# An attention, expert and dense kernel on one core: two column groups share a PSUM bank, and four row loads are issued ahead of seven weight loads

## The chip, the core and the metric

The kernel runs on one core of a Trainium2 chip. The core has five engines with instruction queues of their own: PE (TensorE, the matrix multiplier, whose weight loads are shown apart as PEld), DVE (VectorE), ACT (ScalarE), POOL (GpSimd) and SP (SyncE, which here does nothing but issue DMAs). Each of them takes its instructions in the order in which they were written; they wait for one another through semaphores. [...] The metric is the time of one execution on the device in microseconds (us); of several executions the median is given.

## The reference

Three stages follow each other: attention in chunks, a layer of eight experts with one expert for each row, and a dense layer.

```python
B, H, S, D = 4, 8, 768, 64                 # attention: out[c] = softmax(q_c k_ctx^T / 8) v_ctx
x = attn_out.transpose(0, 2, 1, 3).reshape(3072, 512)
# experts: 8, w1 [512, 1024], w2 [1024, 512]
do = x @ w_skip > 0;  xc = x[do];  e_idx = argmax(xc @ w_gate)
for e in range(8):
    h = np.maximum(xc[mask] @ w1[e], 0.0)
    y[mask] = gate_w[mask, None] * (h @ w2[e])
out[do] = xc + y
# dense: w1, w2, w3 [512, 768], w_out [768, 512]
h = np.maximum(np.maximum(x @ w1, x @ w2), x @ w3)
return h @ w_out
```

## The kernel before

Matmuls take fp32 data as pairs of a rounded part ("hi") and the rest ("lo"): a product a·b is three matmuls, hi·hi, lo·hi and hi·lo. ACT makes the hi part, DVE the lo part, of everything that is multiplied.

**Experts** (`experts`, the loop over e). For each expert up to 256 rows were gathered (POOL, L368) and transposed (`trans`, tiles xh and xl). The first layer makes the 1024 hidden columns in eight groups f of 128 columns. One group is 12 matmuls of 256 rows (L433) into a PSUM tile hp; there are four such tiles (bufs=4), each a bank of 512 columns of which a group uses 256. ACT then writes relu(hp) to hh (L434), and DVE writes what is left to hl (L435), which frees the tile for the group four further on. The second layer (`gemm2`, L454) adds up over f, for two halves h of the rows, into the two yp banks (one buffer each): 6 matmuls of 512 columns for each f, which need hh and hl of that f. In the last expert all f of h=0 come first, then those of h=1, with four transposes of loaded rows (L501, from x0, loaded at L442) between them.

The weights come in 64 pieces of 512 KB, eight for an expert. `K.load` has SP load a piece into one of seven staging tiles (L124, L127) as soon as DVE has released it; `K.split` has ACT cast it to hi (L136) and DVE subtract to lo (L147, wloa or wlob). Splits stand up to five pieces ahead in the program, always before the group f whose matmuls follow them. Twice an expert, at f=2 and f=3, `finish` has DVE add the previous expert's result (L410, reads yp) and POOL scatter it to the rows xn in DRAM (L412). Between all this, `conv` converts 16 pieces ("units") of the dense layer's weights from fp64 on DVE and ACT (L201 to L226, loaded by SP at L189 as craw); seven of them are written to DRAM (tiles away9 to away15, L231), since they don't fit.

**Dense** (`dense`). Rows come in blocks of 512; block 0 was transposed at the end of the experts (x0h, x0l). The kernel computes the hidden layer as gp = product with a unit, max over three units (`first`, L575 to L579), over (block, f) in the order (0,0) (0,1) (0,2) (1,0) (1,1) (1,2) and then block 0 and 1 in turn for f = 3, 4, 5. Block 1 needs its rows: `load` (L550) has SP load 128 rows at a time from xn into the tiles xs, PE transposes them (`trans`, L558), ACT writes dxh (L564) and DVE dxl (L565). These four transposes stand in the code inside (0,1) and (0,2). Units 9 to 15, which f = 3 to 5 use first, are loaded back from DRAM by `C.fetch` (L182). The conversion of units 16 to 23 goes on (L189 and L192 load them), and `sums` builds sums of units on DVE (L622 to L637) for the later blocks.

The order in which SP issues these loads is that of the code: two craw loads, `C.fetch` (seven loads), then `load` of block 1 (four loads).

Of the kernel before, what the change touches and what calls it, by code (L numbers as in the profile page):

```python
# [9 lines left out]
F32 = mybir.dt.float32  # L10
# [4 lines left out]
AF = mybir.ActivationFunctionType  # L15
ALU = mybir.AluOpType
# [336 lines left out]
def order(late):  # L353

    if late:
        return [(c, k) for k in range(4) for c in (0, 1)] + [(2, k) for k in range(4)]
    return [(c, k) for k in range(4) for c in range(3)]
# [16 lines left out]
def experts(ac, tc, nc, env):  # L374
    K, C, tab, xn, ident, gidx, sidx = map(env.__getitem__, ("K", "C", "tab", "xn", "ident", "gidx", "sidx"))
    pool = ac.enter_context(tc.tile_pool(name="ex", bufs=1, reuse_waits="tile"))
    ps = ac.enter_context(tc.tile_pool(name="ex_ps", bufs=2, space=PSUM, reuse_waits="tile"))
# [26 lines left out]
    def passes(ah, al, bh, bl):  # L404
        return ((ah, bh), (ah, bl), (al, bh))
# [3 lines left out]
    def finish(i, y):  # L409
        nc.vector.scalar_tensor_tensor(out=xr[i], in0=y, scalar=tab[:, 1, col(i)], in1=xr[i],  # L410
                                       op0=ALU.mult, op1=ALU.add)
        nc.gpsimd.indirect_dma_start(  # L412
            out=xviews[i], out_offset=bass.IndirectOffsetOnAxis(ap=sidx[:, col(i)], axis=0),
            in_=xr[i], in_offset=None, bounds_check=NT - 1, oob_is_err=False)
# [5 lines left out]
    for e in range(NE):  # L420
        hh = pool.tile([128, 8, 256], F32R, name="hh")
        hl = pool.tile([128, 8, 256], F32R, name="hl")
        for f in range(8):
            if f % 2 == 0:
                i = 8 * e + f // 2
                K.split(2, upto=i + AHEAD)
                K.load()
                wh, wl = (w.rearrange("p (k f) -> p k f", k=4) for w in K.hl[i])
            hp = ps.tile([128, 512], F32, name="hp", bufs=4)
            sl = slice((f % 2) * 128, (f % 2) * 128 + 128)  # L430
            for n, (c, k) in enumerate(order(e == 0 and f == 0)):
                a, b = ((wh, xh[e]), (wl, xh[e]), (wh, xl[e]))[c]
                nc.tensor.matmul(hp[:, 0:256], lhsT=a[:, k, sl], rhs=b[:, k, :], start=(n == 0), stop=(n == 11))  # L433
            nc.scalar.activation(out=hh[:, f, :], in_=hp[:, 0:256], func=AF.Relu)  # L434
            nc.vector.scalar_tensor_tensor(out=hl[:, f, :], in0=hp[:, 0:256], scalar=0.0,  # L435
                                           in1=hh[:, f, :].bitcast(F32), op0=ALU.max, op1=ALU.subtract)
            if f in FIN and done:
                finish(*done.pop(0))
            if e == NE - 1 and f == 4:
                x0 = [xrp.tile([128, DM], F32, name="xr") for _ in range(4)]  # L440
                for t in range(4):
                    nc.sync.dma_start(out=x0[t], in_=xn[t * 128:(t + 1) * 128, :])  # L442
            if f % 2:
                next(conv, None)
                K.free(i)
        if e + 1 < NE:
            trans(e + 1)
        yp = [ps.tile([128, 512], F32, name=f"yp{h}", bufs=1) for h in range(2)]

        def gemm2(f, h):  # L450
            wh, wl = (w.rearrange("p (f d) -> p f d", f=2) for w in K.hl[8 * e + 4 + f // 2])
            sl = slice(h * 128, h * 128 + 128)
            for n, (a, b) in enumerate(passes(hh[:, f, sl], hl[:, f, sl], wh[:, f % 2, :], wl[:, f % 2, :])):
                nc.tensor.matmul(yp[h], lhsT=a, rhs=b, start=(f == 0 and n == 0), stop=(f == 7 and n == 2))  # L454

        if e == NE - 1:
            break
        for f in range(8):
            if f % 2 == 0:
                i = 8 * e + 4 + f // 2  # L460
                K.split(2, upto=i + AHEAD)
                K.load()
                if f == 2 and 1 <= e and e + 2 < NE:
                    gather(nc, xrp, xr, xn, gidx, e + 2)
            for h in range(2):
                gemm2(f, h)
            next(conv, None)
            if f % 2:
                next(conv, None)
                K.free(i)  # L470
        done = [(2 * e + h, yp[h]) for h in range(2)]
# [39 lines left out]
    for h in range(2):  # L511
        for k in range(4):
            for n, w in enumerate((yhi, ylo)):
                nc.tensor.matmul(pk[k], lhsT=w[:, h, k * 128:(k + 1) * 128], rhs=onehot[:, h, :],
                                 start=(h == 0 and n == 0), stop=(h == 1 and n == 1))
# [12 lines left out]
def dense(ac, tc, nc, env):  # L528
# [6 lines left out]
    C, xn, out, ident, dram = map(env.__getitem__, ("C", "xn", "out", "ident", "dram"))  # L535
    V = nc.vector
    pool = ac.enter_context(tc.tile_pool(name="de", bufs=1, reuse_waits="tile"))
    ps = ac.enter_context(tc.tile_pool(name="de_ps", bufs=2, space=PSUM, reuse_waits="tile"))
# [7 lines left out]
    def load(j, t, rows):  # L546

        xs[j, t] = pool.tile([128, 2, DM], F32, name="xs", bufs=3)
        for i, r in enumerate(rows):
            nc.sync.dma_start(out=xs[j, t][:, i], in_=xn[r:r + 128, :])  # L550
# [106 lines left out]
    conv = C.feeder(cpool, range(C.EARLY + C.EXTRA, 24), 0, LP, 1, fine=False)  # L657
    for u in range(C.depth):
        C.load(cpool, C.EARLY + C.EXTRA + u)
    C.fetch()  # L660
    for t in (0, 2):
        load(1, t, (512 + t * 128, 640 + t * 128))
    adds = sums(sp)

    calls = [0]
# [812 lines left out]
```

## Time and profile before

| | us |
|---|---|
| median of 3 executions | 775.68 |
| lowest, highest | 774.61, 780.51 |
| the profiled execution, own time | 779.5 |
| its span (first to last instruction) | 777.8 |
| PE busy | 716.3 (92%) |
| DVE busy | 548.6 (71%) |
| ACT busy | 298.2 (38%) |
| POOL busy | 135.8 (17%) |
| experts' first layer begins | 173.9 |
| dense begins | 383.7 |

The busy shares are means over stages that differ: attention takes the first 170 us, the experts about 210 us, the dense layer the rest. A matmul's row in the trace is longer than its distance to the next one, since matmuls overlap: 12 matmuls of 256 rows start 0.117 us apart. DVE instructions overlap a little too, so that a row's duration is more than what the instruction adds; the distance from start to start tells that. [...]

### The profile page before, as it was taken

What the parts mean: (1) busy time and instruction counts of PE and PEld (TensorE: products, weight loads), DVE (VectorE), ACT (ScalarE), POOL (GpSimd) and SP (SyncE); (2) the same over time, 40 slices, a digit from 0 to 9 for tenths busy, and PEclk for the clock granted to TensorE, in tenths of its full rate; (3) what the DMA queues carried; (4) which work ended last, traced back from release to release, by engine and by line L of the source; (5) the groups of instructions that cost most, each with busy time, mean ns of one, the idle gap of its engine ahead of it and who ended that gap; (6) DMA issues with size and microseconds to landing.
All of it is one profiled execution on the core that took longest, in us unless ns stands there. A gap on an engine that the chain in (4) does not pass through costs nothing.

```text
span 777.8 us, 13743 instructions
## 1 busy us (share of the span) xinstructions
PE 716.3 (92%) x5209; PEld 608.7 (78%) x5209; DVE 548.6 (71%) x1059; ACT 298.2 (38%) x530; POOL 135.8 (17%) x273
## 2 busy tenths in 40 slices
PE   6787988866999999989979999999999999999998
PEld 5666777756998898979757888788888888888876
DVE  5455767865699999999659987455667674666640
ACT  4555755623546655545413322452000163000031
POOL 7334646221022121211101112000000000000000
PEclk8999999968999999999999999999999999999999
DMA  8798999739768878873365676212453231333111
GB/s 215 151 241 211 227 242 207 192 104 328 264 227 274 266 258 279 266 274 116 128 261 190 229 271 230 95 54 95 147 196 145 91 126 54 136 136 135 69 41 67
DMA packets 118548, 140.76 MB, mean 181 GB/s; under 512 B 34574, under 2 KB 84750, under 8 KB 118192
## 3 DMA queue, kind: packets, MB, share of 16 engines
q1 hardware_dynamic: 112608, 121.37, 50.3%
q0 software_dynamic: 5872, 18.49, 6.6%
q8 instruction: 42, 0.69, 0.4%
q14 instruction: 26, 0.21, 0.1%
HBM read 103.30 MB, written 32.24 MB: 174 GB/s over the span
## 4 chain that ended last, share of the span: by engine, by line
PE 50%; DVE 11%; issue 9%; DMA 6%; ACT 1%; POOL 1%; SPq 0%; POOLq 0%; DVEq 0%; ACTq 0%
PE gp L759 22%; PE dtp L605 13%; PE gp L575 10%; DVE wloa L147 2%; PE hp L433 2%; DMA stgb<-in_moe_w_dram 2%; DMA xn<-xr,sidx 2%; DMA xr<-xn,gidx 2%; PE yp L454 1%; DVE hl L435 1%; DVE wlob L147 1%; PE gp L558 1%; DVE cg L207 1%; POOL xn L412 1%; DVE cg L215 1%
## 5 line engine op out<-in xcount | busy, mean ns | idle before, releaser
L763 DVE TENSOR_TENSOR tmp<-tmp,gp 128x512 f32<-128x512 f32 x102 | 70.0, 687 | 49.9 <-PE gp L759 49.7
L605 PE MATMUL dtp<-unit,hp 128*128 128x512 f32 x432 | 101.5, 392 | 1.5 <-DVE hp L590 1.5
L605 PEld LDWEIGHTS dtp<-unit,hp 128*128 128x128 f32 x432 | 80.1, 188 | 19.2 <-DVE hp L590 2.3
L433 PE MATMUL hp<-xh,whia 128*128 128x256 f32 x256 | 74.7, 292 | 12.1 <-DVE hl L435 12.0
L433 PE MATMUL hp<-xh,wloa 128*128 128x256 f32 x256 | 73.7, 288 | 0.0
L433 PE MATMUL hp<-xl,whia 128*128 128x256 f32 x256 | 72.7, 286 | 0.0
L779 ACT COPY tmp<-gp 128x512 f32<-128x512 f32 x18 | 10.6, 588 | 146.4 <-PE gp L759 128.5
L433 PEld LDWEIGHTS hp<-xh,whia 128*128 128x128 f32 x256 | 50.4, 197 | 13.9 <-DVE hl L435 13.7
L454 PE MATMUL yp<-whib,hh 128*128 128x512 f32 x128 | 50.8, 397 | 0.0
L433 PEld LDWEIGHTS hp<-xh,wloa 128*128 128x128 f32 x256 | 50.4, 197 | 0.3
L454 PE MATMUL yp<-whib,hl 128*128 128x512 f32 x128 | 50.0, 390 | 0.0
L454 PE MATMUL yp<-wlob,hh 128*128 128x512 f32 x128 | 49.9, 389 | 0.0
L433 PEld LDWEIGHTS hp<-xl,whia 128*128 128x128 f32 x256 | 49.8, 196 | 0.0
L759 PE MATMUL gp<-unit,set 128*128 128x512 f32 x180 | 46.9, 395 | 0.0
L575 PE MATMUL gp<-x0h,unit 128*128 128x512 f32 x144 | 44.7, 403 | 1.3 <-ACT x0h L520 1.3
L759 PE MATMUL gp<-x0h,unit 128*128 128x512 f32 x144 | 44.5, 390 | 0.0
L575 PE MATMUL gp<-dxh,unit 128*128 128x512 f32 x144 | 44.4, 389 | 0.0
L412 POOL DMA_INDIRECT xn<-xr,sidx x16 | 19.0, 1187 | 136.9 <-DVE xr L410 134.4
L759 PEld LDWEIGHTS gp<-unit,set 128*128 128x128 f32 x180 | 33.7, 187 | 8.2
L590 DVE TENSOR_TENSOR hp<-hm,hp 128x768 fp32r<-128x768 f32 (+2 forms) x26 | 22.9, 896 | 19.8 <-ACT hp L589 19.6
L759 PE MATMUL gp<-unit,unit 128*128 128x512 f32 x144 | 36.6, 389 | 0.0
L434 ACT ACTIVATE hh<-hp 128x256 fp32r<-128x256 f32 x64 | 23.3, 384 | 32.8 <-PE hp L433 30.3
(272 smaller groups left out, 1646.1 us busy)
## 6 DMA issues: line engine op xcount, KB each, us to landing
stga<-in_moe_w_dram SPq DMA_DIRECT2D x38, 512.0 KB
stgb<-in_moe_w_dram SPq DMA_DIRECT2D x26, 512.0 KB
set<-sum SPq DMA_DIRECT2D x20, 512.0 KB
craw<-in_moe_w_dram SPq DMA_DIRECT2D x18, 512.0 KB
unit<-sum SPq DMA_DIRECT2D x16, 512.0 KB
k<-in_k_dram SPq DMA_DIRECT2D x12, 512.0 KB
q<-in_q_dram SPq DMA_DIRECT2D x12, 512.0 KB
out_dram<-ob SPq DMA_DIRECT2D x24, 256.0 KB
```

What stands on the lines that cost most here:

```text
L147: self.nc.vector.tensor_tensor(out=lo, in0=t, in1=hi.bitcast(F32), op=ALU.subtract)
L207: V.scalar_tensor_tensor(out=gu, in0=Hw, scalar=0x80000000, in1=gu, op0=ALU.bitwise_and, op1=ALU.bitwise_or)
L412: nc.gpsimd.indirect_dma_start(out=xviews[i], out_offset=bass.IndirectOffsetOnAxis(ap=sidx[:, col(i)], axis=0), in_=xr[i], in_offset=None, ...
L433: nc.tensor.matmul(hp[:, 0:256], lhsT=a[:, k, sl], rhs=b[:, k, :], start=(n == 0), stop=(n == 11))
L434: nc.scalar.activation(out=hh[:, f, :], in_=hp[:, 0:256], func=AF.Relu)
L454: nc.tensor.matmul(yp[h], lhsT=a, rhs=b, start=(f == 0 and n == 0), stop=(f == 7 and n == 2))
L575: nc.tensor.matmul(gp[w], lhsT=l_[:, k, :], rhs=r_[:, k, :], start=(n == 0), stop=(n == 11))
L590: V.tensor_tensor(out=p[:, 1, F], in0=m, in1=p[:, 0, F].bitcast(F32), op=ALU.subtract)
L605: nc.tensor.matmul(op, lhsT=l_, rhs=r_, start=(f == 0 and c == 0), stop=(f == 5 and c == 2))
L759: nc.tensor.matmul(acc, lhsT=l_[:, i, :], rhs=r_[:, i, :], start=(n == 0), stop=(n == 5))
L763: V.tensor_tensor(out=o, in0=x, in1=y, op=ALU.add)
L779: nc.scalar.copy(u, m1)
```

## The change

Two edits, with nothing else moved.

First, a PSUM tile hp now takes the groups f and f+1 of a pair: the tile is made at even f, group f writes half f % 2, and after the odd group one ACT and one DVE instruction of 512 columns do what four of 256 did. The four tiles therefore hold eight groups, a whole first layer. Second, in `dense`, the four loads of block 1's rows stand before `C.fetch` in the code.

```diff
-            hp = ps.tile([128, 512], F32, name="hp", bufs=4)
+                hp = ps.tile([128, 2, 256], F32, name="hp", bufs=4)
             sl = slice((f % 2) * 128, (f % 2) * 128 + 128)
             for n, (c, k) in enumerate(order(e == 0 and f == 0)):
                 a, b = ((wh, xh[e]), (wl, xh[e]), (wh, xl[e]))[c]
-                nc.tensor.matmul(hp[:, 0:256], lhsT=a[:, k, sl], rhs=b[:, k, :], start=(n == 0), stop=(n == 11))
-            nc.scalar.activation(out=hh[:, f, :], in_=hp[:, 0:256], func=AF.Relu)
-            nc.vector.scalar_tensor_tensor(out=hl[:, f, :], in0=hp[:, 0:256], scalar=0.0,
-                                           in1=hh[:, f, :].bitcast(F32), op0=ALU.max, op1=ALU.subtract)
+                nc.tensor.matmul(hp[:, f % 2], lhsT=a[:, k, sl], rhs=b[:, k, :], start=(n == 0), stop=(n == 11))
+            if f % 2:
+                F = slice(f - 1, f + 1)
+                nc.scalar.activation(out=hh[:, F], in_=hp, func=AF.Relu)
+                nc.vector.scalar_tensor_tensor(out=hl[:, F], in0=hp, scalar=0.0, in1=hh[:, F].bitcast(F32),
+                                               op0=ALU.max, op1=ALU.subtract)
 ...
-    C.fetch()
     for t in (0, 2):
         load(1, t, (512 + t * 128, 640 + t * 128))
+    C.fetch()
```

On PE and POOL the instructions and their order are the same. On ACT and DVE 64 instructions become 32. The DVE queue of the first expert, from the split of its fifth piece on, reads before:

```order
L147 TENSOR_TENSOR wlob_3187<-stga_79,whib_3186 128x1024
L435 SCALAR_TENSOR_TENSOR hl<-hp,hh 128x256 x2
L147 TENSOR_TENSOR wlob_3189<-stga_80,whib_3188 128x1024
L147 TENSOR_TENSOR wlob_3191<-stgb_3183,whib_3190 128x1024
L435 SCALAR_TENSOR_TENSOR hl<-hp,hh 128x256 x2
L147 TENSOR_TENSOR wlob_3193<-stgb_3184,whib_3192 128x1024
L435 SCALAR_TENSOR_TENSOR hl<-hp,hh 128x256 x2
L147 TENSOR_TENSOR wloa_84<-stgb_3185,whia_83 128x1024
L435 SCALAR_TENSOR_TENSOR hl<-hp,hh 128x256 x2
L399 TENSOR_TENSOR xl<-tp,xh 128x4x128 x2
L147 TENSOR_TENSOR wloa_86<-stga_81,whia_85 128x1024
```

The same place in the kernel after, from the same split on:

```order
L147 TENSOR_TENSOR wlob_3187<-stga_79,whib_3186 128x1024
L437 SCALAR_TENSOR_TENSOR hl<-hp,hh 128x512
L147 TENSOR_TENSOR wlob_3189<-stga_80,whib_3188 128x1024
L147 TENSOR_TENSOR wlob_3191<-stgb_3183,whib_3190 128x1024
L437 SCALAR_TENSOR_TENSOR hl<-hp,hh 128x512
L147 TENSOR_TENSOR wlob_3193<-stgb_3184,whib_3192 128x1024
L437 SCALAR_TENSOR_TENSOR hl<-hp,hh 128x512
L147 TENSOR_TENSOR wloa_84<-stgb_3185,whia_83 128x1024
L437 SCALAR_TENSOR_TENSOR hl<-hp,hh 128x512
L399 TENSOR_TENSOR xl<-tp,xh 128x4x128 x2
L147 TENSOR_TENSOR wloa_86<-stga_81,whia_85 128x1024
```

No instruction changed places with another: each pair of hl writes became one, and the splits still stand between them.

SP's queue where the dense layer begins, before, from the last craw loads of the experts' stage to the first of w_out (unit and away carry the buffer numbers of the seven units):

```order
L189 DMA craw<-in_moe_w_dram 128x4x256 x2
L182 DMA unit_5332<-away_3159 128x1024
L182 DMA unit_5333<-away_3160 128x1024
L182 DMA unit_5334<-away_3161 128x1024
L182 DMA unit_5335<-away_3162 128x1024
L182 DMA unit_5336<-away_3163 128x1024
L182 DMA unit_5337<-away_3164 128x1024
L182 DMA unit_5338<-away_3165 128x1024
L550 DMA xs<-xn 128x512 x4
L192 DMA craw<-in_moe_w_out_dram 128x1024 x4
```

And after:

```order
L189 DMA craw<-in_moe_w_dram 128x4x256 x2
L552 DMA xs<-xn 128x512 x4
L182 DMA unit_5236<-away_3159 128x1024
L182 DMA unit_5237<-away_3160 128x1024
L182 DMA unit_5238<-away_3161 128x1024
L182 DMA unit_5239<-away_3162 128x1024
L182 DMA unit_5240<-away_3163 128x1024
L182 DMA unit_5241<-away_3164 128x1024
L182 DMA unit_5242<-away_3165 128x1024
L192 DMA craw<-in_moe_w_out_dram 128x1024 x4
```

The four xs loads moved ahead of the seven unit loads; the craw loads of w_out (units 18 and on) stay behind both.

## Rows read from the trace of the kernel before

**Rows 1.** Windows: start:end length, PE, PEld, DVE, ACT, POOL busy, clock, DMA share, GB/s.

```profile
200.00:340.00 140.00, 134.19 (x871) 122.42 (x871) 130.11 (x203) 77.44 (x126) 27.25 (x22) 0.99 0.82 272
```

**Rows 2.** Waits in 174 to 400: engine line, releaser, us, times, longest.

```profile
PE hp L433 <- DVE hl L435: 12.0, 7, 4.5
```

**Rows 3.** Timeline of PE, experts: start, us, ..., idle before and its releaser.

```profile
182.01 0.39 PE L433 MATMUL hp<-xh,whia 128*128 128x256 f32 x1 [1.62 <-DVE hl L435]
...
189.61 0.58 PE L433 MATMUL hp<-xh,whia 128*128 128x256 f32 x1 [4.53 <-DVE hl L435]
...
334.78 0.39 PE L433 MATMUL hp<-xh,whia 128*128 128x256 f32 x1 [3.04 <-DVE hl L435]
...
370.87 0.60 PE L501 MATMUL tp<-ident,xr 128*128 128x128 f32 x4
```

**Rows 4.** Windows behind two of these waits.

```profile
189.60:195.20 5.60, 5.59 (x26) 5.59 (x27) 3.64 (x6) 1.80 (x5) 0.00 (x0) 0.50 1.06 378
...
334.00:340.00 6.00, 5.22 (x31) 5.22 (x32) 6.00 (x11) 0.95 (x3) 1.63 (x2) 0.72 0.96 327
```

**Rows 5.** Timeline of ACT in the first expert.

```profile
186.92 1.04 ACT L136 CAST whib<-stgb 128x1024 fp32r<-128x1024 f32 x1 [2.75 <-DMA stgb<-in_moe_w_dram]
```

**Rows 6.** Timeline of DVE, experts.

```profile
189.14 0.75 DVE L435 SCALAR_TENSOR_TENSOR hl<-hp,hh 128x256 fp32r<-128x256 f32 x2
189.80 1.22 DVE L147 TENSOR_TENSOR wlob<-stgb,whib 128x1024 fp32r<-128x1024 f32 x1
...
191.60 1.22 DVE L147 TENSOR_TENSOR wloa<-stgb,whia 128x1024 fp32r<-128x1024 f32 x1
...
195.55 0.42 DVE L435 SCALAR_TENSOR_TENSOR hl<-hp,hh 128x256 fp32r<-128x256 f32 x1 [2.14 <-ACT hh L434]
...
198.01 1.23 DVE L147 TENSOR_TENSOR wloa<-stga,whia 128x1024 fp32r<-128x1024 f32 x1
...
204.73 0.43 DVE L203 TENSOR_SCALAR cg<-cg 128x512 f32<-128x512 f32 x1 [3.22 <-ACT cg L201]
...
366.60 0.74 DVE L435 SCALAR_TENSOR_TENSOR hl<-hp,hh 128x256 fp32r<-128x256 f32 x2
```

**Rows 7.** Timeline of SP: DMA issues.

```profile
199.70 1.04 SPq L189 DMA_DIRECT2D craw<-in_moe_w_dram  x2
...
366.95 1.75 SPq L442 DMA_DIRECT2D xr<-xn  x4
...
386.55 3.26 SPq L182 DMA_DIRECT2D unit<-away  x7
395.15 1.89 SPq L550 DMA_DIRECT2D xs<-xn  x4
397.15 0.36 SPq L192 DMA_DIRECT2D craw<-in_moe_w_out_dram  x1
```

**Rows 8.** Timeline of POOL: the second scatters of the seventh and the eighth expert.

```profile
364.27 1.42 POOL L412 DMA_INDIRECT xn<-xr,sidx  x1 [0.30 <-issue]
...
388.74 0.99 POOL L412 DMA_INDIRECT xn<-xr,sidx  x1 [0.31 <-issue]
```

**Rows 9.** Timeline where block 1 is transposed: PE, DVE, ACT.

```profile
400.06 0.64 PE L558 MATMUL dtp<-ident,xs 128*128 128x128 f32 x4 [4.84 <-DMA xs<-xn]
...
419.53 0.50 PE L575 MATMUL gp<-dxl,unit 128*128 128x512 f32 x1 [1.67 <-DVE dxl L565]
...
401.36 0.69 DVE L565 TENSOR_TENSOR dxl<-dtp,dxh 128x512 fp32r<-128x512 f32 x1 [3.07 <-ACT dxh L564]
...
405.08 0.69 DVE L579 TENSOR_TENSOR hm<-hm,gp 128x512 f32<-128x512 f32 x1 [3.03 <-PE gp L575]
405.69 0.42 DVE L203 TENSOR_SCALAR cg<-cg 128x512 f32<-128x512 f32 x1
...
418.79 0.69 DVE L565 TENSOR_TENSOR dxl<-dtp,dxh 128x512 fp32r<-128x512 f32 x1
...
412.31 0.68 ACT L201 ACTIVATE cg<-craw 128x512 f32<-128x512 f32 x1
```

## Prediction

> **What bounds the kernel now.** I read the windows by stage first. From 200 to 340 us, most of the experts, PE is busy for 134 of 140 us and DVE for 130 [rows 1]: two engines near full, so the next question is which waits for which. The list of waits shows PE waiting for hl, that is for a free hp tile, for 12.0 us in seven waits [rows 2]; DVE hardly waits for PE there. So DVE sets the pace, and it reaches PE through the four hp tiles. The timeline of PE puts most of the sum in two places: 1.62 and 4.53 us in the first expert and 3.04 us in the seventh [rows 3]. The first has a price beyond the wait: behind the wait of 4.53 us the granted clock is 0.50 from 189.6 to 195.2 [rows 4], where 24 matmuls take 5.6 us; at full clock they take 24 x 0.117 = 2.8 us. After the wait of 3.04 us the clock is again below full (0.72 over 334 to 340, the wait included [rows 4]).
>
> Why was hl late? In the first expert ACT waits for a piece of weights (2.75 us, until 186.92 [rows 5]), DVE's subtraction of that piece stands ahead of hl(2,3) in the queue, and hl(2,3) runs at 189.14 [rows 6], though its hp groups were long done. A late load stops PE through a buffer that has nothing to do with that load.
>
> The second place is the start of the dense layer. PE waits 4.84 us for xs [rows 9]. SP issues xs at 395.15, though its seven unit loads were out by 386.55 + 3.26 = 389.8 [rows 7]: in between it waits for the last scatter, issued at 388.74 [rows 8], 6.4 us earlier. The scatter before, issued at 364.27, let SP go on at 366.95 [rows 7, 8]: 2.7 us. The difference is what else was moving: seven 512 KB loads at 388, none at 364. DVE waits behind PE, 3.07 us for dxh and 3.03 us for gp [rows 9], and then runs without a pause to dxl of the fourth transpose (418.79 to 419.48), on which PE waits a last time, 1.67 us [rows 9].
>
> **Edit 1, the shared bank.** *The waits on hp go.* With eight groups in four tiles, the tile for pair j of the next expert was read long before. What PE waits for is now hl itself, in the second layer, and there it is needed later. In the first expert PE would go on at 182.01 - 1.62 = 180.4 [rows 3] and end the first layer 4 x 12 x 0.117 = 5.6 us later, at 186.0. It needs hl(2,3), still at 189.14 to about 189.8, only after eight transposes (about 1 us) and two f of `gemm2` (12 matmuls of 512 columns, 0.23 us each: 2.7 us), at 189.7. Nothing is left of the waits and of the slow clock: PE gains 1.6 + 4.5 + 2.8 = 8.9 us there, and 16 us over the stage with the other five waits. But DVE, which sets the pace, doesn't gain that.
>
> *What DVE gains at the start.* It waits for ACT, and through it for PE, at the last hl of the first expert (2.14 us, to 195.55), and reaches the next split at 198.01 [rows 6]. Without that: split from 191.60 to 192.7, hl(6,7) to 193.3, two xl of 0.6 to 194.5. So 198.01 becomes 194.5, 3.5 us. DVE then stops for craw until 204.73 (3.22 us) [rows 6]; those two loads were issued at 199.70 [rows 7], right behind the staging tile that the split at 198.01 released, so they move with it. Bounds: 3.5 if the loads follow; nothing if the DMA engines are full (share 1.06 over 189.6 to 195.2 [rows 4], 0.82 over 200 to 340 [rows 1]). I take 3.5, since a release, not a transfer, held these issues.
>
> *What the merged instructions save.* From start to start two hl of 256 columns take 189.80 - 189.14 = 0.66 us [rows 6]; the wide one is bounded by the nearest row, hm<-hm,gp, which reads 512 columns of PSUM too: 405.69 - 405.08 = 0.61 [rows 9]. It saves 0.05 to 0.07, 0.06 x 32 = 1.9 us. The durations alone (0.42 twice against 0.69) would say 4.8 us; they overlap, and it is the starts that count. [...] ACT saves about as little and isn't full; the cost is that hh of an even group comes a group (1.4 us) later, hidden because DVE lags PE by more than that.
>
> *The end.* In the last expert hl(6,7) ends at 367.34 [rows 6]. PE, then ahead, does f = 6, 7 of h = 0 in 1.36 us and wants the first x0 transpose: 368.7 in times of before, against 370.87 [rows 3]. The x0 rows, issued at 366.95 [rows 7], allow about 369.6 if they land as fast as the quiet scatter (2.7 us; an estimate). So PE gains 1.3 us on DVE. Together 3.5 + 1.9 + 1.3 = 6.7 us. Bounds: 3.2 without the start; 8.5 if DVE's waits for ACT that stem from PE go as well. The lead of 16 us is not the limit.
>
> **Edit 2, xs first.** SP issues xs as soon as the scatter lands: 388.74 + 2.7 = 391.4 (times of before), 3.7 us earlier, and no unit load is ahead of them. They land by about 394.5 to 395; PE gets to its transpose at 400.06 - 4.84 = 395.2. That wait goes, and with it both of DVE's, 6.1 us. From then on DVE is the bound, so dxl of the fourth transpose comes 6.1 us earlier. PE, at full clock, wants it 1.2 us earlier still than that wait allows and waits about 2.9 us instead of 1.67; if the clock falls after it, as after 3.04 us [rows 4], (1 - 0.72) x 5.2 = 1.5 us are lost again. I take half of that, 6.1 - 0.8 = 5.3; bounds 2.5 (below) and 6.1. The units land some 7 us later, at about 404; f = 3 wants them after six calls of 36 matmuls, 6 x 36 x 0.23 = 50 us behind 383.7: those calls hide the later landing, which would cost its own length otherwise. Queued behind them is craw of unit 18. It was issued at 397.15 [rows 7] and is wanted by ACT at 412.31 [rows 9], that is 406.2 now; behind 1 MB of xs and 3.67 MB of units at about 0.4 MB/us it lands at about 407. A microsecond of ACT, which the tolerance of two gp tiles each hides.
>
> **Sum.** 6.7 + 5.3 = 12.0 us. Against the profiled execution's own 779.5 that is 767.5; it is a slow one of the kind, 3.8 us over the median of 775.68, and from the median it is 763.7. Some of those 3.8 us may sit in waits that go anyway, so I take the middle, **765.5**.
>
> **The rivals.**
> *Loads hold the experts.* If the DMA engines, full in the first expert, keep craw where it was, DVE's 3.5 us are lost; the rest is 8.5, 769.0. For it: share 1.06 [rows 4]; against it: 0.82 afterwards.
> *The scatter isn't quicker.* If its 6.4 us are its own, SP issues xs at 395.15 as before, and only the transfer is faster: 2.5 us instead of 5.3, 768.3. Against it stands the scatter of 2.7 us. [...] With both of these: about 771.8.
> *Nothing moves.* If DVE's work alone sets the experts' end and xs is only hidden elsewhere, 1.9 + 1 us, 774.
> *Slower.* craw of unit 18 now stands behind seven loads. ACT takes its queue in order, and behind that instruction stand the copies of gp and dxh; a late craw would stop ACT, then DVE, then PE. Each microsecond beyond 406.2 costs one, less about 2 of tolerance. It takes 12 + 2 us to turn the sign: craw at 420, twice the transfer time of everything ahead of it; at 430 the kernel would be at 785. In rows 4 the engines move 327 to 378 GB/s, so I give it little.
>
> **How the numbers follow.** Chances: forecast 0.55 (759 to 768, by the bounds of its terms), loads 0.17, scatter 0.11, both 0.07, nothing 0.05, slower 0.05. A difference of 1% (7.8 us, 767.9) is about what a measurement can tell. Under it lie nearly all of the forecast and some of the single rivals: faster 0.65, same 0.30, slower 0.05. The range that leaves out no more than 2 in 10, from the forecast's lower end to the double rival: 759 to 772.
>
> **What the profile after would show.** Edit 1: no wait of PE on an hp tile; clock 1.00 through 180 to 200; the second layer of the first expert from about 187 instead of 196; short waits of PE in `gemm2` on hl; DVE as full as before. Wide hl rows of 0.69 us that add about 0.61. Edit 2: from scatter to xs under 3 us, no wait on xs, DVE without its two pauses, a wait of up to 3 us on dxl. It is wrong if DVE's second split of the second expert isn't earlier, if xs still waits 6 us for the scatter, or if ACT waits for craw at unit 18.

## The result and the profile after

| | before | after |
|---|---|---|
| median of 6 executions, us | 775.78 | 769.24 |
| lowest, highest | 773.69, 780.51 | 764.52, 770.75 |
| the profiled execution, own time | 779.5 | 766.06 |
| its span | 777.8 | 764.3 |

The ratio is 0.9892, with a 95% interval from 0.985 to 0.9934: 8.4 us less by the ratio, 6.5 by the medians. The interval excludes that nothing changed, but not a gain of less than 1%. The forecast was 765.5, in a range of 759 to 772; of that range the forecast's own terms cover 759 to 768, and 769.24 lies above them, where the prediction had put its single rivals. On another chip the same kernel took 768.3 us against 775.79 (0.9889, 0.9856 to 0.9922).

Lines of the code stand two further down from the edit on (L436 for hh, L437 for hl, L456 for `gemm2`, L552 for xs, L577 for gp). The waits of PE in 174 to 400 us (engine line, releaser: us, times, longest) answer to [rows 2]:

```profile
PE yp L456 <- DVE xr L410: 5.8, 8, 3.5
PE gp L577 <- ACT x0h L522: 1.3, 1, 1.3
PE tp L503 <- DMA xr<-xn: 1.1, 1, 1.1
```

The waits on hp are gone. In their place PE waits in `gemm2` for the bank yp, which `finish` (L410) has to have read. The windows (columns as in [rows 1]) show the first expert, the middle, and the seventh expert:

```profile
180.00:200.00 20.00, 20.00 (x129) 18.09 (x128) 12.94 (x14) 10.05 (x14) 0.00 (x0) 1.00 1.04 369
200.00:340.00 140.00, 134.16 (x868) 120.27 (x867) 131.31 (x185) 78.48 (x110) 25.77 (x22) 0.99 0.83 274
332.50:338.50 6.00, 5.91 (x19) 4.52 (x20) 6.00 (x9) 3.70 (x6) 2.68 (x2) 0.72 0.92 315
```

The clock is 1.00 through the first expert, where it was 0.50 behind the long wait [rows 4]. The middle looks as before [rows 1]: PE 134 of 140 us, DVE 131. The seventh expert still has a wait and a clock of 0.72. The timeline of PE at the first `gemm2` of the first expert, in the seventh, at the x0 transposes, and in block 1:

```profile
186.35 0.48 PE L456 MATMUL yp<-whib,hh 128*128 128x512 f32 x1
...
332.59 0.61 PE L456 MATMUL yp<-whib,hh 128*128 128x512 f32 x1 [3.48 <-DVE xr L410]
...
363.24 0.63 PE L503 MATMUL tp<-ident,xr 128*128 128x128 f32 x4 [1.13 <-DMA xr<-xn]
...
387.48 0.60 PE L560 MATMUL dtp<-ident,xs 128*128 128x128 f32 x4
...
406.14 0.50 PE L577 MATMUL gp<-dxl,unit 128*128 128x512 f32 x1 [2.47 <-DVE dxl L567]
```

The wait of 4.84 us on xs [rows 9] is gone, that on dxl went from 1.67 to 2.47. The timeline of DVE, with the wide hl, the splits of the second expert, the stop for craw, and the last hl:

```profile
187.85 0.68 DVE L437 SCALAR_TENSOR_TENSOR hl<-hp,hh 128x512 fp32r<-128x512 f32 x1
188.46 1.21 DVE L147 TENSOR_TENSOR wlob<-stgb,whib 128x1024 fp32r<-128x1024 f32 x1
...
193.12 3.48 DVE L147 TENSOR_TENSOR wloa<-stga,whia 128x1024 fp32r<-128x1024 f32 x3
201.53 0.43 DVE L203 TENSOR_SCALAR cg<-cg 128x512 f32<-128x512 f32 x1 [4.93 <-ACT cg L201]
...
360.21 0.67 DVE L437 SCALAR_TENSOR_TENSOR hl<-hp,hh 128x512 fp32r<-128x512 f32 x1
```

From start to start the wide hl takes 188.46 - 187.85 = 0.61 us. The queues, SP and POOL:

```profile
194.79 1.04 SPq L189 DMA_DIRECT2D craw<-in_moe_w_dram  x2
...
383.45 1.76 SPq L552 DMA_DIRECT2D xs<-xn  x4
385.32 3.94 SPq L182 DMA_DIRECT2D unit<-away  x7
```
```profile
381.15 0.99 POOL L412 DMA_INDIRECT xn<-xr,sidx  x1 [0.30 <-issue]
```

xs is issued 383.45 - 381.15 = 2.3 us after the last scatter; it was 6.4 [rows 7, 8].

For a ledger, take the experts from the first matmul of the first layer to the first of the dense layer, cut where the third and the seventh expert begin, then the dense start up to the end of PE's wait on dxl, and the rest of the span. All times are starts of PE's rows; e1 to e12 are the experiments below.

| us | experts 1, 2 | 3 to 6 | 7, 8 | experts | dense start | rest |
|---|---|---|---|---|---|---|
| before | 56.2 | 95.9 | 57.8 | 209.8 | 35.8 | 358.2 |
| before, second trace (e11) | 53.7 | 95.7 | 59.7 | 209.0 | 36.3 | 358.3 |
| after | 48.8 | 95.0 | 59.3 | 203.1 | 30.0 | 358.2 |
| after, second trace (e8) | 48.6 | 95.1 | 60.1 | 203.7 | 29.7 | 358.2 |
| e1 bank only | 48.8 | 95.0 | 59.7 | 203.5 | 35.4 | 358.3 |
| e2 rows first only | 55.1 | 95.7 | 58.0 | 208.7 | 30.0 | 359.9 |
| e3 narrow | 53.8 | 105.8 | 66.3 | 225.9 | 29.5 | 359.9 |
| e4 two banks | 53.0 | 95.5 | 58.4 | 206.9 | 29.5 | 358.2 |
| e5 narrow in turn | 48.7 | 95.9 | 58.8 | 203.4 | 29.6 | 359.8 |
| e6 fetch late | 48.6 | 95.0 | 58.5 | 202.1 | 29.5 | 358.3 |
| e7 cx places | 49.1 | 95.0 | 59.2 | 203.3 | 30.4 | 359.8 |
| e9 both places | 48.7 | 95.0 | 56.8 | 200.5 | 30.9 | 359.9 |
| e10 both places, fetch late | 48.5 | 95.7 | 56.7 | 200.8 | 29.5 | 358.2 |
| e12 three ahead | 48.6 | 95.0 | 59.2 | 202.8 | 30.7 | 358.2 |

By PE's starts the gain is made in experts 1 and 2 (4.8 to 7.6 us by the pairs of before and after), 0.6 to 0.9 come from 3 to 6, and in 7 and 8 it goes from 0.4 gained to 2.3 given back. The dense start gains 5.8 to 6.7.

Part of the first figure is only a lead: PE now runs further ahead of DVE, and gives that up again by the end. DVE's own queue tells them apart. Its split of the third expert's first piece (the 17th of 64), before and after:

```profile
219.43 1.22 DVE L147 TENSOR_TENSOR wloa<-stga,whia 128x1024 fp32r<-128x1024 f32 x1
```
```profile
214.55 1.21 DVE L147 TENSOR_TENSOR wloa<-stga,whia 128x1024 fp32r<-128x1024 f32 x1
```

That is 45.5 us behind the first matmul of the layer before, and 41.6 after; the second traces have 43.0 and 41.3. Up to there DVE gained 1.4 to 4.2 us. Its last writes of hl start 192.7 and 191.8 us behind the first matmul before [rows 6], 187.2 and 187.5 after: 4.3 to 5.5 us.

The rest of the span has two lengths, 1.6 us apart. The clock behind the wait on dxl tells them apart: the window of six us behind it, in the changed kernel (wait 2.47) and in e2 (wait 2.49):

```profile
406.10:412.10 6.00, 5.96 (x26) 4.96 (x27) 5.65 (x9) 2.19 (x4) 1.79 (x3) 1.00 0.68 246
```
```profile
411.90:417.90 6.00, 5.97 (x19) 4.79 (x20) 4.07 (x7) 2.17 (x4) 1.78 (x3) 0.72 0.70 245
```

All five traces with a rest of 359.8 or 359.9 have 0.72 there, all nine with 358.2 or 358.3 have 1.00. Where the wait is 1.67 or 1.69 us (before, e11, e1, e12) the clock never fell; with 2.0 to 3.4 us it fell in five of ten, and at 2.0 to 2.1 as well as at 2.5.

### The profile page after: what moved, and what is told of

Same layout as the page of the kernel before. It is cut to its first block, busy times and chain, and to the rows that moved or that the text cites. A ratio compares the mean times of both kernels' runs of the same rounds, so it can differ in the third digit from the quotient of the medians.

```text
span 764.3 us, 13711 instructions
## 1 busy us (share of the span) xinstructions
PE 707.9 (93%) x5209; PEld 598.6 (78%) x5209; DVE 546.2 (71%) x1027; ACT 292.6 (38%) x498; POOL 133.5 (17%) x273
## 4 chain that ended last, share of the span: by engine, by line
PE 46%; issue 13%; DMA 11%; DVE 5%; POOL 2%; ACT 1%; SPq 0%; POOLq 0%; DVEq 0%; ACTq 0%
PE gp L761 23%; PE dtp L607 13%; PE gp L577 10%; DMA xr<-xn,gidx 4%; DMA xn<-xr,sidx 3%; DMA craw<-in_moe_w_out_dram 1%; DMA stgb<-in_moe_w_dram 1%; POOL xn L412 1%; DVE wloa L147 1%; PE gp L560 1%; DVE wlob L147 1%; DMA craw<-in_moe_w_dram 1%; DVE hl L437 1%; DMA xs<-xn 1%; DVE xr L410 0%
## 5 line engine op out<-in xcount | busy, mean ns | idle before, releaser
L433 PE MATMUL hp<-xh,whia 128*128 128x256 f32 x256 | 72.2, 282 | 0.0
L433 PE MATMUL hp<-xh,wloa 128*128 128x256 f32 x256 | 72.0, 281 | 0.0
L456 PE MATMUL yp<-whib,hh 128*128 128x512 f32 x128 | 52.1, 407 | 5.8 <-DVE xr L410 5.8
L456 PE MATMUL yp<-wlob,hh 128*128 128x512 f32 x128 | 50.7, 396 | 0.0
L456 PE MATMUL yp<-whib,hl 128*128 128x512 f32 x128 | 50.5, 395 | 0.0
L433 PEld LDWEIGHTS hp<-xh,whia 128*128 128x128 f32 x256 | 48.8, 191 | 0.3
L433 PEld LDWEIGHTS hp<-xh,wloa 128*128 128x128 f32 x256 | 48.7, 190 | 0.3
L577 PE MATMUL gp<-x0h,unit 128*128 128x512 f32 x144 | 43.5, 393 | 1.3 <-ACT x0h L522 1.3
L577 PE MATMUL gp<-dxh,unit 128*128 128x512 f32 x144 | 44.4, 389 | 0.0
L1043 PE MATMUL xp<-vs,pb 128*64 128x65 f32 x736 | 28.0, 230 | 10.2 <-DMA vs<-vs 2.7
```

The lines of the kernel that those rows point to most:

```text
L433: nc.tensor.matmul(hp[:, f % 2], lhsT=a[:, k, sl], rhs=b[:, k, :], start=(n == 0), stop=(n == 11))
L577: nc.tensor.matmul(gp[w], lhsT=l_[:, k, :], rhs=r_[:, k, :], start=(n == 0), stop=(n == 11))
L1043: nc.tensor.matmul(xps[t][hd // 4][cp * 64:cp * 64 + 64, (hd % 4) * (D + 1):(hd % 4 + 1) * (D + 1)], lhsT=pb[:, hd // 2, cp, hd % 2, :], r ...
```

## The experiments

Each kernel was timed in five rounds beside the kernel before, unless said otherwise; in the three groups before had medians of 777.25, 775.79 and 778.8 us, so kernels of different groups are compared by their ratios to it.

**e1, the bank only.** The changed kernel with the loads in the old order:

```diff
+    C.fetch()
     for t in (0, 2):
         load(1, t, (512 + t * 128, 640 + t * 128))
-    C.fetch()
```

> The kernel before with the shared bank alone; the seven unit loads stay ahead of xs. Theory (the two edits gain apart, about 6.7 and 5.8 us of the stage): the experts, from the first matmul of the first layer to the first of the dense layer, last about 203 us instead of 209.8; the dense layer still needs about 36 us from its first matmul to the end of the wait on dxl, with a wait of some 5 us on xs; the time is 6 to 7 us below that of before. Rival (the bank's gain shows only together with xs, since PE's lead is spent at the next wait): the experts are shorter but the wait on xs grows by as much, and the time is within 2 us of before.

Measured: 772.37 us, ratio 0.993 (0.9906 to 0.9954), 4.9 us less, where 6 to 7 were expected and the rival said under 2; experts 203.5, dense start 35.4. PE waits for xs as before:

```profile
393.73 1.08 PE L560 MATMUL dtp<-ident,xs 128*128 128x128 f32 x4 [4.48 <-DMA xs<-xn]
```

**e2, the rows first only.** The kernel before with the second hunk of the change alone.

> The kernel before with the order of the loads alone; hp as before. Theory: the experts last 209.8 us as before with PE's seven waits on hl; the scatter of block 0 lands in 2 to 3 us instead of 6.4, PE has no wait on xs, and the dense layer reaches the end of the wait on dxl 30 us after its first matmul instead of 36; 5 to 6 us below before. Rival (the scatter is slow by itself, or its quickness in the changed kernel came from the experts that end earlier): xs is issued 6 us after the scatter, and the gain is under 3 us.

Measured: 773.53 us, ratio 0.9947 (0.9925 to 0.9969), 3.7 us less, where 5 to 6 were expected and the rival said under 3; experts 208.7, dense start 30.0. The second scatter was issued at 386.94:

```profile
389.23 1.76 SPq L550 DMA_DIRECT2D xs<-xn  x4
```

So 2.3 us again, although these experts are as long as before: the quicker scatter comes from the order of the loads alone. The two edits gain apart from each other: about 6 us each in their stages, 4.9 and 3.7 in the medians, together 8.6. In this trace of e2 the clock behind dxl took 1.6 us back.

**e3, narrow instructions.** The shared bank, but each group is read by instructions of its own, in the order ACT, DVE, ACT, DVE:

```diff
-                nc.scalar.activation(out=hh[:, F], in_=hp, func=AF.Relu)
...
+                for g in (f - 1, f):
+                    nc.scalar.activation(out=hh[:, g], in_=hp[:, g % 2], func=AF.Relu)
+                    nc.vector.scalar_tensor_tensor(out=hl[:, g], in0=hp[:, g % 2], scalar=0.0,
+                                                   in1=hh[:, g].bitcast(F32), op0=ALU.max, op1=ALU.subtract)
```

> The changed kernel, but hh and hl are written by two instructions of 256 columns each, one behind the other, after the odd group of the bank: eight groups of look-ahead stay, the merging of instructions goes. Theory (it is the starts that count, 0.06 us for a pair, 32 pairs): the experts last 2 us longer than in the changed kernel (205 against 203.1), the time is 1.5 to 2.5 us over it. Rival (each instruction costs its fixed part or its whole duration of 0.42 us): 5 us over it. Second rival (DVE doesn't set the pace): the same time within 0.5 us.

Measured: 790.76 us, ratio 1.0155 (1.0131 to 1.018): 13.5 us more than before. None of the three expectations. The waits of ACT and of PE in 174 to 395 us, and one of the 32 on the timeline of ACT:

```profile
ACT hh L437 <- DVE hl L438: 66.0, 32, 4.5
...
PE yp L457 <- DVE xr L410: 19.9, 12, 5.1
```
```profile
211.69 0.38 ACT L437 ACTIVATE hh<-hp 128x256 fp32r<-128x256 f32 x1
214.07 0.38 ACT L437 ACTIVATE hh<-hp 128x256 fp32r<-128x256 f32 x1 [2.00 <-DVE hl L438]
```

ACT's second read of a bank waited until DVE's first read of the same bank was over, though the columns differ: 32 times, 66.0 us. DVE in turn waited for ACT's second hh (14.4 us in 32 waits), so the two engines took turns on every bank where they had worked side by side on two (before, DVE waits for hh twice, 2.3 us, and ACT never for hl); both fell back, and with them `finish`, for which PE stood 19.9 us. What makes ACT wait was not tested further. In this order two groups in a bank don't pay (1.0155); with merged instructions (0.9892) or in another order of narrow ones (e5, 0.9903) they do.

**e4, two banks.** The pairs rotate over two banks instead of four, which is the old look-ahead of four groups, though now freed in pairs, with merged instructions:

```diff
...
-                hp = ps.tile([128, 2, 256], F32, name="hp", bufs=4)
+                hp = ps.tile([128, 2, 256], F32, name="hq", bufs=2)
...
```

> The changed kernel, but the pairs rotate over two banks instead of four: four groups of look-ahead, as before the change, with the merged instructions (the other two banks only take the warming matmuls and the last products of the experts). Theory (the look-ahead brings the 3.5 us at the start and the 1.3 at the end, the merging 1.9): PE waits on the bank for hl again, above all 3 to 5 us with half clock in the first expert, and the experts last 206 to 208 us; 3 to 5 us over the changed kernel. Rival (merging is what gains): 203 us and the same time as the changed kernel.

Measured: 772.8 us, ratio 0.994 (0.9916 to 0.9964); experts 206.9. PE waits for hl again, 10.2 us in seven waits, of which the longest stands in the first expert:

```profile
182.98 0.38 PE L433 MATMUL hq<-xh,whia 128*128 128x256 f32 x1 [3.54 <-DVE hl L437]
```

The size is the theory's: of the 6 us of gain in the experts, some 3.5 (206.9 against 203.1 and 203.7) hang on the look-ahead. The place is not. By PE's starts they lie in experts 1 and 2 (53.0 against 48.7), but that is lead again: DVE's stop for craw, the last hl, and PE's first x0 transpose in e4 are

```profile
202.50 0.43 DVE L203 TENSOR_SCALAR cg<-cg 128x512 f32<-128x512 f32 x1 [4.51 <-ACT cg L201]
...
362.94 0.69 DVE L437 SCALAR_TENSOR_TENSOR hl<-hq,hh 128x512 fp32r<-128x512 f32 x1 [0.16 <-ACT hh L436]
```
```profile
367.59 0.60 PE L503 MATMUL tp<-ident,xr 128*128 128x128 f32 x4
```

With the first matmul at 173.6 the stop ends 28.9 us behind it, against 28.5 in the changed kernel, and the 17th split starts 41.9 us behind it, against 41.6. DVE's start therefore loses 0.4 us without the longer look-ahead, not 3.5. The last hl comes 189.3 us behind the first matmul, against 187.2, and the x0 transpose 4.7 us behind that hl, against 3.0: the look-ahead pays in the last experts and at the end.

**e5, narrow in turn.** As e3, but both hh of a bank ahead of both hl:

```diff
+                for g in (f - 1, f):
+                    nc.scalar.activation(out=hh[:, g], in_=hp[:, g % 2], func=AF.Relu)
+                for g in (f - 1, f):
+                    nc.vector.scalar_tensor_tensor(out=hl[:, g], in0=hp[:, g % 2], scalar=0.0,
+                                                   in1=hh[:, g].bitcast(F32), op0=ALU.max, op1=ALU.subtract)
```

> The changed kernel, hh and hl again by instructions of 256 columns, but in another order than in the first narrow version: both hh of a bank, then both hl. There ACT's second hh waited for DVE's first hl each time (66 us in 32 waits), so that version measured a wait and not the price of an instruction. Theory (two starts cost 0.06 us more than one, and DVE sets the pace): no such waits of ACT; the experts last about 205 us against 203.1 in the changed kernel, 1.5 to 2.5 us over it. Rival (fixed cost of an instruction, or the whole duration): 5 us over it. Second rival (the bank is shared by the two engines in turn even so, ACT behind DVE from pair to pair): 10 us or more over it.

Measured: 769.73 us, ratio 0.9903 (0.9869 to 0.9937), against 768.3 for the changed kernel in the same group (e8): 1.4 us more, with intervals that overlap, so that the time alone doesn't tell the theory from no difference; it speaks against both rivals. Experts 3 to 6, where nothing but DVE's work sets the length, take 95.9 us against 95.1: 0.86 for four experts, or 0.21 for one, where 4 pairs of 0.06 were expected, 0.24. In the whole of the experts (203.4 against an expected 205, and against 203.1 and 203.7) it doesn't show: experts 7 and 8 were 1.3 us shorter here than in e8, where DVE stood 3.2 us for ACT behind the store that e7 is about, and here 1.9.

**e6, the weights later still.** `C.fetch` stands behind the call (0,2), three calls later:

```diff
-    C.fetch()
...
+        if (j, f) == (0, 2):
+            C.fetch()
```

> The changed kernel with the seven unit loads issued three calls later still, behind the craw loads of units 18 to 20. Theory (ACT's wait of 1.49 us for craw of unit 18, which stands behind the seven loads, is part of what makes dxl late): that wait goes, the wait of 2.47 us on dxl becomes about 1 us, from the first matmul of the dense layer to the end of the wait 28.5 us instead of 30.0; 1 to 1.5 us below the changed kernel. Rival (dxl waits for DVE's own work): 30 us as before, no difference.

Measured: 766.64 us, ratio 0.9869 (0.9834 to 0.9903), 1.7 us under the changed kernel, with intervals that overlap. The timeline of ACT in the changed kernel, and of ACT and PE in e6:

```profile
400.02 0.68 ACT L201 ACTIVATE cg<-craw 128x512 f32<-128x512 f32 x1 [1.49 <-DMA craw<-in_moe_w_out_dram]
```
```profile
399.14 0.67 ACT L201 ACTIVATE cg<-craw 128x512 f32<-128x512 f32 x1
...
406.37 0.50 PE L577 MATMUL gp<-dxl,unit 128*128 128x512 f32 x1 [2.00 <-DVE dxl L567]
```

ACT's wait is gone as expected, the wait on dxl is not: the dense start is 29.5 us against 30.0 and 29.7. The wait on dxl comes mostly from DVE's own work. So the lateness of craw costs 0.1 to 0.5 us; the rest of the 1.7 lies in the experts, whose code is the same (202.1 us here), and can't be put down to this edit.

**e7, places for cx.** Seen in the trace after: before the wait of 3.48 us ACT stands 6.73 us, until the store of cx to DRAM has left its single buffer. SP's issue of the store and ACT's wait:

```profile
315.02 0.46 SPq L231 DMA_DIRECT2D away<-cx  x1
```
```profile
322.11 0.62 ACT L225 CAST cx<-cg 128x512 fp32r<-128x512 f32 x1 [6.73 <-DMA away<-cx]
```

The kernel before has the same wait, ahead of PE's 3.04 us on hp [rows 3]; whether it is the cause there was not tested:

```profile
326.76 0.62 ACT L225 CAST cx<-cg 128x512 fp32r<-128x512 f32 x1 [4.99 <-DMA away<-cx]
```

e7 gives the high parts of the seven stored units places of their own, in the memory of x0h and x0l:

```diff
+        C.spare = [x[:, k] for x in x0 for k in range(4)]
...
-            hi, lo = pool.tile([128, 512], F32R, name="cx", bufs=1), g.bitcast(F32R)
+            hi, lo = self.spare[u - self.EARLY], g.bitcast(F32R)
```

> The changed kernel, but the seven units that go to DRAM take their high parts from seven places of their own (the memory of x0h and x0l, unused until the last expert ends) instead of one cx buffer. Theory (the wait of PE of 3.48 us on the bank of the second layer in the seventh expert, and the slow clock after it, stem from ACT's wait of 6.73 us until cx has left for DRAM): both go, the experts last 199 to 201 us instead of 203.1; 2 to 4 us below the changed kernel. Rival (DVE's own work sets the end, the lateness is made up elsewhere): experts 203, no difference.

Measured: 769.85 us, ratio 0.9908 (0.9875 to 0.9941): no gain. The timeline of ACT and PE in e7:

```profile
322.64 0.67 ACT L202 ACTIVATE cg<-craw 128x512 f32<-128x512 f32 x1 [2.24 <-DMA away<-cg]
...
332.50 0.58 PE L457 MATMUL yp<-whib,hh 128*128 128x512 f32 x1 [3.40 <-DVE xr L411]
```

The wait moved one instruction on, to the buffer cg, from which the low part is stored, and ended at the same time.

**e9, places for both parts.** Four pairs of places, the low part too:

```diff
...
-            hi, lo = pool.tile([128, 512], F32R, name="cx", bufs=1), g.bitcast(F32R)
+            n = 2 * ((u - self.EARLY) % 4)
+            hi, lo = self.spare[n:n + 2]
...
-            for c, x in enumerate((hi, g)):
+            for c, x in enumerate((hi, lo)):
```

> The changed kernel with four pairs of places of their own (the memory of x0h and x0l) for the high and the low part of a unit that goes to DRAM. With places for the high part alone ACT's wait moved one instruction on, to cg<-craw, whose cg buffer was still on its way to DRAM (2.24 us until 322.64; whib after it as late as before). Theory (the stores to DRAM, which take 7 us there, reach PE through ACT, DVE and the bank of the second layer): now ACT has neither wait, the subtraction of whib starts at 321.5 instead of 324.3, PE's wait of 3.4 us in the seventh expert falls to 1 us or less without slow clock behind it, the experts last 200 to 201.5 us instead of 203.1 to 203.7; 2 to 3 us below the changed kernel (768.3). Rival (another of the waits in this place takes over, such as the load of the next weights): PE's wait stays over 2 us, no difference.

Measured: 767.18 us, ratio 0.9847 (0.9821 to 0.9874); experts 200.5. The wait of PE in the seventh expert, and the window behind it in the changed kernel and in e9:

```profile
332.76 0.47 PE L458 MATMUL yp<-whib,hh 128*128 128x512 f32 x1 [0.90 <-DVE xr L412]
```
```profile
330.00:340.00 10.00, 7.41 (x25) 5.75 (x26) 10.00 (x14) 5.47 (x8) 2.68 (x2) 0.83 0.86 303
```
```profile
330.00:340.00 10.00, 8.86 (x47) 7.14 (x46) 10.00 (x14) 5.48 (x8) 2.68 (x2) 1.00 0.89 313
```

DVE's subtraction of whib, in the changed kernel and in e9:

```profile
324.38 1.23 DVE L147 TENSOR_TENSOR wlob<-stga,whib 128x1024 fp32r<-128x1024 f32 x1 [0.93 <-ACT whib L136]
```
```profile
324.54 1.23 DVE L148 TENSOR_TENSOR wlob<-stga,whib 128x1024 fp32r<-128x1024 f32 x1 [0.47 <-ACT whib L137]
```

The first matmul of the layer stands at 173.0 in the changed kernel's trace and at 175.9 in e9's, so that 324.54 is 321.6 in times of the former: the 321.5 that were expected. PE's wait of 0.90 us, the clock of 1.00 and the 200.5 us came as expected too. The chain is shown: the stores, issued at 315.02 and gone at 322.1 in the trace after, held ACT, then DVE's subtractions, then `finish`, then PE. The time is 0.4% below the changed kernel by the ratios, with intervals that overlap.

**e10, both places and the weights later.** The edits of e6 and e9 together.

> The kernel of the run above with the seven unit loads three calls later. Theory: both gains add up, experts 200 to 201.5 us, dense start 29.5 us, the time 764 to 766 us, below the changed kernel by 2 to 4. Rival: as the late loads alone, 766.6 us.

Measured: 764.67 us (762.6 to 765.53), ratio 0.9813 (0.979 to 0.9835). Experts 200.8, dense start 29.5. This kernel beats both, before by 1.9% and the changed one (0.9889 and 0.9892) by some 0.8%. In e9 ACT waited 2.39 us for craw in the dense start, and PE 3.4 us for dxl; with the weights later the dense start is 1.4 us shorter. That the two gains add up is borne out.

**e11, before once more.** One execution, 780.55 us.

> The kernel before once more, for a second trace. The changed kernel gained 12.5 us in the two stages of the profiled runs, 7 to 8.4 us in the medians. Theory (the first profiled run of before, 779.5 us, had longer waits in these stages than most): experts 206 to 208.5 us instead of 209.8 and a dense start of 34 to 35.5 us at a time of 774 to 777. Rival (the stages are always as long, and the difference lies before the experts or behind the dense start): experts 209.5 to 210, dense start 35.8, and at 774 to 777 us the first layer starts 3 us earlier than in the first trace, or the rest is 3 us shorter.

The waits of PE in it, in 170 to 420 us:

```profile
PE hp L433 <- DVE hl L435: 11.2, 6, 3.7
PE dtp L558 <- DMA xs<-xn: 4.9, 1, 4.9
```

Experts 209.0, dense start 36.3, almost the first trace. But this execution too was long, so it does not say how the stages look in one of 775 us. Inside the experts the two differ: experts 1 and 2 took 2.5 us less, 7 and 8 1.9 us more.

**e12, three loads ahead.** Three of the seven unit loads (1.57 MB) ahead of xs, four behind; one execution, 770.37 us.

```diff
...
+    C.fetch(slice(0, 3))
     for t in (0, 2):
         load(1, t, (512 + t * 128, 640 + t * 128))
-    C.fetch()
+    C.fetch(slice(3, 7))
```

> The changed kernel with three of the seven unit loads ahead of xs and four behind. Theory (a scatter's end comes after what the loads ahead of it move: 3.67 MB 6.4 us, none 2.1 to 2.7): 1.57 MB give a landing of about 4 us, xs is issued about 4 us after the last scatter, PE waits 0 to 1 us for xs, and the dense start takes 30 to 31 us. Rival (any load ahead costs the whole): 6 us and 35 us. Second rival (the scatter is slow only with more loads than the queue takes): 2 to 2.7 us, 30 us.

Measured: xs is issued 389.80 - 384.73 = 5.1 us after the scatter, PE waits 1.26 us, the dense start takes 30.7. The timeline of SP and POOL:

```profile
382.55 1.29 SPq L182 DMA_DIRECT2D unit<-away  x3
389.80 1.75 SPq L552 DMA_DIRECT2D xs<-xn  x4
```
```profile
384.73 0.99 POOL L412 DMA_INDIRECT xn<-xr,sidx  x1 [0.30 <-issue]
```

The scatter and the wait lie above the theory (about 4 us, and 0 to 1), the dense start lies in its range; neither rival came. No load ahead gives 2.3 us, three give 5.1, and the order of before gives 6.4 and 6.9 (before, e1). In that order SP issues a load every 0.47 us from 386.55 on [rows 7], so that five of the seven were out when the scatter was issued at 388.74 [rows 8], and all seven when POOL's instruction had ended. Above 2.3 us the three loads cost 0.9 us each; five would cost 0.8 to 0.9 each, seven 0.6 to 0.7. So in these runs the end of the scatter went with the loads that were out; whether in proportion, the runs don't settle, since they don't say how many of the seven count.

## Why the prediction was right, and where it was not

**The waits on hp go: right.** None is left, and the clock stays at 1.00 through 180 to 200 us. `gemm2` of the first expert starts at 186.35, forecast at about 187.

**PE then waits for hl: wrong.** It waits for yp, 5.8 us in eight waits. Both halves of the result have one bank each, and `finish` stands in DVE's queue among the next expert's first layer; a PE that runs ahead meets this limit first. The prediction counted the lead of 16 us as free (by its own rows it is 12.0 + 2.8 = 14.8) and never asked which other buffer PE would run into. It cost little in most experts, and in the seventh 3.5 us, with a clock of 0.72 over the six us behind it.

**The start, 3.5 us: too much.** From the first matmul to the end of DVE's stop for craw it is 28.5 and 28.3 us after, 30.8 and 29.2 before (first and second trace): 0.7 to 2.6 us gained. The split and the loads behind it came earlier as forecast (the loads at 194.79 instead of 199.70), but ACT had craw 6.0 us after their issue, where it took 4.3 before (5.7 and 5.3 in the second traces). The timeline of ACT, before and after:

```profile
204.03 0.67 ACT L201 ACTIVATE cg<-craw 128x512 f32<-128x512 f32 x1 [4.16 <-DMA craw<-in_moe_w_dram]
```
```profile
200.83 0.67 ACT L201 ACTIVATE cg<-craw 128x512 f32<-128x512 f32 x1 [6.69 <-DMA craw<-in_moe_w_dram]
```

The step that was wrong is "a release, not a transfer, held these issues": the release moved, and the transfer took back part of it. In this stretch the DMA engines were full (share 1.04 over 180 to 200 us). That is the rival "loads hold the experts", which the prediction gave 0.17; it takes 0.9 to 2.8 of the 3.5 us. That the full engines are the reason was not tested by a run. Nor does the gain at the start need eight groups of look-ahead: e4, with four, has its stop end at 28.9 us.

**The merged instructions, 0.06 us a pair: right, as far as it shows.** e5 gives 0.21 us for an expert in experts 3 to 6; carried over to eight that is 1.7, and the term was 1.9. In the stage as a whole it doesn't show. The 4.8 us by the durations alone, 32 x (2 x 0.42 - 0.69) [rows 6, 9], are not borne out, nor are the 5 us that the rivals of e3 and e5 give an instruction's fixed part or whole duration: e5 took 1.4 us more.

**The end, 1.3 us: right, and with the bound that was named.** The x0 transposes begin at 363.24, after a wait of 1.13 us on xr (the list above has it with 1.1); hl(6,7) starts at 360.21 and 3.0 us lie between, against 370.87 - 366.60 = 4.3 before [rows 3, 6].

**The experts, 6.7 us.** The traces give 5.3 to 6.7, by their pairs, 6.0 in the mean. That the sum came out is in part luck. DVE's start brought less than its term. The store of cx took some back in the seventh expert: between the 49th and the 53rd split DVE is idle for 2.9 and 3.4 us after, 1.4 and 2.2 before, and 0.6 in e9. The prediction listed PE's 3.04 us there [rows 3] and didn't ask what stood behind it. What made up for both are shorter waits of DVE in experts 2, 7 and 8, of the kind that the prediction had only in its upper bound of 8.5: from the 13th to the 17th and from the 53rd to the 61st split DVE is idle for 3.3 and 3.4 us before, 1.4 us in both traces after. In e4, with the old look-ahead, DVE is idle for 0.1 us in the first of these stretches and 2.6 in the second, so that only the second hangs on the look-ahead.

**The dense start, 5.3 us: right; the half was a guess that came out.** Up to the end of the wait the traces give 5.8 to 6.7. The scatter lands in 2.3 us (2.7 was the estimate), the transposes have no wait, ACT waits 1.49 us for craw as forecast (about 1), and that costs 0.1 to 0.5 (e6). The prediction charged half of 1.5 us for a fall of the clock behind a wait of about 2.9 on dxl. The wait was 2.1 to 2.5, and the fall costs 1.6. It comes in five of the ten traces with a wait of 2.0 us or more, though in neither of the two of the changed kernel itself: 6.2 - 0.8 = 5.4 in the mean.

**From the sum to the median: the step that failed.** The sum of 12.0 us came true between the traces, by 11.9 to 12.5 us in the two stages (their times: 779.5 and 780.55 before, 766.06 and 767.6 after). The medians moved by 6.5 to 8.4. The prediction saw that the profiled execution lay 3.8 us over the median and took the middle, 765.5. Of the 12.0 us the medians lack 3.6 to 5.5, as much as the whole 3.8 or more, where the prediction took off half. Both traced executions of before are longer than most: of eleven in the second group seven lie between 773.4 and 776.6, four between 778.0 and 781.02. Both traced executions of after had no fall of the clock behind dxl; with one they would be 1.6 us longer, which is one part of the gap. The other part is on the side of before: where its shorter executions save 4 or 5 us stays open, since none was traced. That the waits which the change removes vary fits it (experts 1 and 2 differ by 2.5 us between two executions that are 1 us apart), but was not shown.

**The rival of 769.0.** The median of 769.24 is what "loads hold the experts" would give. What it describes was there, with 0.9 to 2.8 of the 3.5 us; but the experts as a whole gained what was forecast or little less, so that the agreement of the totals is no proof of it.

## What to carry to other kernels

When a buffer is made deeper, list the next buffer that the faster engine meets, and price the wait there; here it was yp, one bank with its reader in a busy queue. In these runs two groups shared a PSUM bank at little cost only where ACT and DVE didn't take turns on it (in turns 1.0155); merged instructions (0.9892), or both reads of one engine ahead of both of the other (0.9903), did that. Where one engine sets the pace, measure a gain at that engine: an engine with a lead shows lead and gain together. And a gain that is read from one profiled execution should be forecast against executions of that length: take a second trace, or price only what both have.

## What the runs showed of the hardware

- A scatter of 128 rows let SP go on after 2.3 us with no unit loads ahead of it, 5.1 us with three, 6.4 and 6.9 in the order of before, where five of seven were out at its issue.
- The same wait, with the same work around it, had its clock fall in one trace and not in another: 0.72 over six us behind 2.49 us (e2), 1.00 behind 2.47 (after). It costs 1.6 us of an execution (the two lengths of the rest). Behind 3.4 and 3.5 us in the seventh expert (e7, after) the matmuls stood 0.43 us apart until 336 us (in after at a clock of 0.52 over 332.6 to 336.1), and 0.23 after.
- Executions of one kernel on one chip differ by up to 7.6 us (773.47 to 781.02). Between traces the first matmul of the experts starts at 172.8 to 178.4 us, before anything that the change touches.
